# The first scores and the product with w_in of two row halves, issued head by head in turn, in a fused attention, SoLU and expert kernel

## The chip, the cores and the metric

The kernel runs on one core of one Trainium2 chip. The metric is the device time of one execution in microseconds (us). The core has TensorE (PE, with its weight loads as PEld), VectorE (DVE), ScalarE (ACT), GpSimd (POOL) and SyncE (SP, which issues the transfers).

## The reference

Eight batches of eight heads of attention, in which 32 packed queries per head first attend to 576 keys, and the 576 tokens then attend to the 32 packed values; a dense layer with a SoLU and a layer norm; and a layer of eight experts of which each token takes one.

```python
def sm_attn(qq, kk, vv):
    s = scale * np.matmul(qq, kk.transpose(0, 1, 3, 2))
    s = s - np.max(s, axis=-1, keepdims=True)
    a = np.exp(s)
    a = a / (np.sum(a, axis=-1, keepdims=True) + 1e-09)
    return np.matmul(a, vv)
p_packed = sm_attn(p, k, v)           # [8, 8, 32, 64]
out = sm_attn(q, p_packed, p_packed)  # [8, 8, 576, 64]
...
h = x @ w_in                          # [4608, 512] @ [512, 1024]
...
return (ln @ w_out).astype(np.float32)
...
xe = x[mask]
h = np.maximum(xe @ w1[e], 0.0)
ye = h @ w2[e]
out[mask] = gate_w[mask, None] * ye
```

## The kernel before

The program has two parts. The first does attention, the dense layer and the gate, batch by batch; the second does the experts. The change touches the first part alone.

Each batch is a row of steps, and every step is a function with a letter: `P` (`packed`) computes the first scores, their softmax and the packed values; `S` (`scores2`) the second scores; `W` (`w_keys`) multiplies the packed values by w_in, so that the hidden units follow from the second softmax directly; `A` (`attnT`) transposes that softmax; `H` (`hidden`) makes the hidden units of a tile of 128 tokens and their norm; `T` (`lnT`) transposes them; `X` (`second`) multiplies by w_out; `G` (`gate`) picks the expert. A string of letters sets the order in which the steps are written, with P, S, W and A one batch ahead. In the first batch the steps `F`, `I` and `D` are mixed in: they fetch w_in and w_out as float64 words and decode them to float32 on ScalarE, VectorE and GpSimd (lines 105 to 123 and 154 to 156).

The written order is not the order on the engines: the program is built with a scheduler (`schedule_with_timeline_sim=True`, at the end) that moves instructions within each engine's stream when the program is built. On the chip each engine takes its stream in that order.

The eight heads of a batch are split in two halves: heads 0 to 3 lie on the lower 64 partitions and heads 4 to 7 on the upper 64 (`g` is the half, `c` the head in it). In the first scores a matmul takes 64 rows and 32 columns (the 32 packed queries of one head), and writes 32 partitions of the accumulator: the four heads of a half fill its 128 partitions. So one group is four matmuls, each with 288 of the 576 keys; `hf` is the half of the keys. The product with w_in is built alike, with 512 of 1024 columns in a group. A float32 matmul appears in the trace as two matmuls and two weight loads, so a group is 8 rows of each.

The accumulator (PSUM) is shared out in pools. `psa` has two tiles of one bank and serves the first scores, their transposes, the packed values, the second scores, the product with w_in and the gate. `psh` has two tiles of two banks (tag `h`) and serves the hidden units alone. A new tile of a pool waits until the last reader of the tile that it replaces is done.

In `packed` a half g takes two tiles of psa for its scores (one for each half of the keys). Each has a maximum of its own (line 172), the two are merged (line 174), and two exponentials with a sum each follow (line 178); then the transposes (line 184) and their copies to SBUF (lines 185 and 188). The second half begins when the first is through. In `w_keys` each group has a tile of psa, and is copied twice (lines 219 and 220) into a rounded and a remainder part.

Of the kernel before, what the change touches and what calls it, by code (L numbers as in the profile page):

```python
# [12 lines left out]
F32 = mybir.dt.float32  # L13
# [5 lines left out]
# The upper word of 2^-127, the float64 whose exponent is 0 in float32, as float32 bits.  # L19
F64_LEAST = float(np.array(0x38000000, np.uint32).view(np.float32))  # L20
AF = mybir.ActivationFunctionType
ALU = mybir.AluOpType
AX = mybir.AxisListType
# [3 lines left out]
B, H, S, D, NP = 8, 8, 576, 64, 32  # L27
DM, FF, E, FF2 = 512, 1024, 8, 1024
P = 128
NC = 4          # heads of one half of the partitions; also chunks of 128 in DM  # L30
NF = FF // P    # chunks of 128 in FF (and in FF2)
# [6 lines left out]
def f32(ap):  # L38
    return ap.bitcast(F32)
# [3 lines left out]
def fused_kernel(ctx: ExitStack, tc, qT, kT, pT, vm, vt, w_in, w_out, g_ln, w_gate, w1, w2, out):  # L43
# [21 lines left out]
    # ------------------------------------------------------------ attention and the first layer  # L65
    with ExitStack() as ph:
# [23 lines left out]
        # Buffers of later steps in which the 16 blocks of the two float64 arrays are decoded,  # L90
        # and whether GpSimd multiplies their lower words.
# [3 lines left out]
        def fetch(src, i):  # L95
            """Words of float64 values, with room to decode them: [P, pairs | pairs, 512]."""
            tag = room[i]
            if tag == "e":
                raw = p4.tile([P, 2, 512], I32, name=f"raw{i}", tag="e")
                t = p4.tile([P, 2, 512], I32, name=f"bits{i}", tag="e")  # L100
            else:
                both = p1.tile([P, 2, 2, 512], I32, name=f"raw{i}", tag=tag)
                raw, t = both[:, 0], both[:, 1]
            raw = raw.rearrange("p t n -> p (t n)")
            SY.dma_start(raw.bitcast(I64), src)
            return raw.rearrange("p (n w) -> p n w", w=2), t

        def decode(dst, words, through_pool):
            """dst = the float64 values as float32."""
            w, t = words  # L110
            lo, hi = w[:, :, 0], w[:, :, 1]
            a, b2 = t[:, 0], t[:, 1]
            A.activation(f32(a), f32(hi), AF.Abs)
            V.tensor_scalar(f32(a), f32(a), F64_LEAST, None, op0=ALU.max)
            V.tensor_scalar(b2, a, 3, 0x3FFFFFFF, op0=ALU.logical_shift_left, op1=ALU.bitwise_and)
            V.scalar_tensor_tensor(a, hi, -0x40000000, b2, op0=ALU.bitwise_and, op1=ALU.bitwise_or)  # L116
            V.tensor_scalar(b2, a, -0x800000, None, op0=ALU.bitwise_and)
            if through_pool:
                A.activation(f32(lo), lo.bitcast(U32), AF.Copy, scale=2.0**-52)
                G.tensor_tensor(f32(b2), f32(lo), f32(b2), op=ALU.mult)  # L120
            else:
                V.scalar_tensor_tensor(f32(b2), lo.bitcast(U32), 2.0**-52, f32(b2), op0=ALU.mult, op1=ALU.mult)
            G.tensor_tensor(dst, f32(a), f32(b2), op=ALU.add)
# [34 lines left out]
        def packed(b):  # L158
            """The packed values of every head, [k, d], by 4 heads on the partitions."""
            s = st[b]  # L160
            rz = sm.tile([P, 2], F32, name=f"rz_{b}", tag="rz")
            a1T = pa.tile([P, NT, 2, P], F32, name=f"a1T_{b}", tag="a1T")
            for g in range(2):
                r = slice(g * 64, g * 64 + 64)
                nm = sm.tile([P, 2], F32, name=f"nm_{b}_{g}", tag="nm")
                pss = []
                for hf in range(2):
                    ps = psa.tile([P, 512], F32, name=f"s1_{b}_{g}_{hf}", tag="a")
                    for c in range(NC):
                        T.matmul(ps[c * NP : (c + 1) * NP, :HALF], s["p"][r, c, :],  # L170
                                 s["k"][r, c, hf * HALF : (hf + 1) * HALF], start=True, stop=True)
                    V.tensor_reduce(nm[:, hf : hf + 1], ps[:, :HALF], axis=AX.X, op=ALU.max, negate=True)
                    pss.append(ps)
                V.tensor_tensor(nm[:, 0:1], nm[:, 0:1], nm[:, 1:2], op=ALU.min)
                a = p2.tile([P, S], F32, name=f"a1_{b}_{g}", tag="a1")
                z = sm.tile([P, 2], F32, name=f"z_{b}_{g}", tag="z")
                for hf in range(2):
                    A.activation(a[:, hf * HALF : (hf + 1) * HALF], pss[hf][:, :HALF], AF.Exp, bias=nm[:, 0:1],
                                 accum_out=z[:, hf : hf + 1])
                V.scalar_tensor_tensor(z[:, 0:1], z[:, 0:1], 1e-9, z[:, 1:2], op0=ALU.add, op1=ALU.add)  # L180
                V.reciprocal(rz[:, g : g + 1], z[:, 0:1])
# [25 lines left out]
        def w_keys(b):  # L207
            """The packed values times w_in."""
            s = st[b]
            s["wb_hi"] = pa.tile([P, 2, FF], F32R, name=f"wbh_{b}", tag="wbh")  # L210
            s["wb_lo"] = pa.tile([P, 2, FF], F32R, name=f"wbl_{b}", tag="wbl")
            for hf in range(2):
                for g in range(2):
                    r = slice(g * 64, g * 64 + 64)
                    cols = slice(hf * 512, hf * 512 + 512)
                    ps = psa.tile([P, 512], F32, name=f"wb_{b}_{g}_{hf}", tag="a")
                    for c in range(NC):
                        T.matmul(ps[c * NP : (c + 1) * NP, :], s["pp"][r, c, :], w_in_sb[r, c, cols], start=True, stop=True)  # L218
                    A.copy(s["wb_hi"][:, g, cols], ps)
                    V.tensor_sub(s["wb_lo"][:, g, cols], ps, f32(s["wb_hi"][:, g, cols]))  # L220
# [44 lines left out]
        def hidden(b, t):  # L265
            """Hidden units of a tile of tokens, their SoLU and its layer norm (w_out carries the gain).

            With u = exp(h - max) h / FF and Z the softmax's denominator, SoLU is u FF / Z:
            its norm is (u - mean u) (var u + 1e-6 (Z / FF)^2) ^ -0.5.
            """  # L270
# [30 lines left out]
        def lnT(b, t):  # L301
# [8 lines left out]
            for f0 in (0, 4):  # L310
                # No other step of the first batch needs psx so early.
# [79 lines left out]
        # A step of the orders below is its letter, its part and, in the first one, a + for batch 1.  # L391
# [10 lines left out]
        # Every batch overlaps the first steps of the next one and the last steps of the one before.  # L402
# [7 lines left out]
    # ------------------------------------------------------------ the experts  # L410
    with ExitStack() as ph:
# [31 lines left out]
        def expert(xh, xl, b, e, emit, nm, split=()):  # L443
            """The terms of expert e for the tokens of batch b; emit(dc, halves, sums, weights) takes them.

            In the chunks of split one half of the tokens is done before the other.
            """
# [35 lines left out]
        # Each batch with the expert of its first token.  # L483
# [12 lines left out]
        # Where a token of any batch goes to another expert, its weight there is zero:  # L496
        # then all batches are computed again with all experts.
# [57 lines left out]
```

## Time and profile before

| | |
|---|---|
| time, median of 3 runs | 968.62 us (967.9 to 969.72) |
| profiled execution, span from first to last instruction | 967.9 us |
| TensorE busy | 915.5 us, 95% |
| VectorE, ScalarE, GpSimd busy | 56%, 42%, 13% |
| first part ends, second part begins | about 570 us |

The span of the profiled execution and the lowest of the three runs are the same to 0.1 us. A busy TensorE is not TensorE at its peak: matmuls overlap, so the time of a piece of work is read from its first start to the start of what comes next. The names of tiles in the trace are cut: `s` stands for first and second scores (lines 170 and 231), `wb` for the product with w_in, `a` for a softmax, `nm` for the maxima of the first scores, `lt` for the transposes of the hidden units, `x` for the product with w_out.

### The profile page before, as it was taken

Reading aid. Unit: us, or ns where it says so; the run is one execution under the profiler, and the core shown is the slowest. Engines: PE = TensorE matmul, PEld = TensorE weight load, DVE = VectorE, ACT = ScalarE, POOL = GpSimd, SP = SyncE. Lnnn points to the kernel's source line nnn. Section 1 sums busy time; section 2 is a strip of 40 time slices with the busy share of each in tenths; the row PEclk is TensorE's granted clock in tenths of the full one; section 3 lists DMA queues with packets and bytes.
Section 4 is the critical chain, followed back from the end, with each engine's and each line's share of the span. In section 5 each row is a group of like instructions: output and inputs, shape, how many; then the busy total and the mean of one; then the engine's idle time right before and its main releaser. Section 6 shows DMA issues by size and latency. Waiting matters only on the chain.

```text
span 967.9 us, 18591 instructions
## 1 busy us (share of the span) xinstructions
PE 915.5 (95%) x7480; PEld 807.3 (83%) x7480; DVE 539.3 (56%) x1090; ACT 402.2 (42%) x800; POOL 124.2 (13%) x228
## 2 busy tenths in 40 slices
PE   4466999999999999999999999999999999999997
PEld 1234777887878878788788999999999999999997
DVE  5999758575575756757456243353434353535331
ACT  4447555444554446444345241333323232324230
POOL 2776312011120101101010000000000000000000
PEclk9988999999999999999999999999999999999999
DMA  9613113022221222200106235353535353433411
GB/s 341 244 45 123 50 56 145 14 90 100 102 98 40 82 82 98 99 2 2 50 1 225 78 116 166 99 175 90 182 99 174 102 173 103 149 127 100 132 46 52
DMA packets 42506, 102.89 MB, mean 106 GB/s; under 512 B 4592, under 2 KB 14384, under 8 KB 38320
## 3 DMA queue, kind: packets, MB, share of 16 engines
q1 hardware_dynamic: 42416, 101.65, 31.1%
q8 instruction: 61, 1.00, 0.4%
q14 instruction: 29, 0.24, 0.1%
HBM read 82.60 MB, written 19.04 MB: 105 GB/s over the span
## 4 chain that ended last, share of the span: by engine, by line
PE 87%; DVE 6%; DMA 2%; ACT 1%; issue 1%; SPq 1%; POOL 0%; DVEq 0%; ACTq 0%
PE y L476 21%; PE x L331 21%; PE h L458 21%; PE h L279 11%; PE lt L315 3%; PE wb L218 2%; PE s L170 2%; PE s L231 2%; PE lg L342 1%; PE pp L193 1%; PE at L260 1%; DMA raw_0a<-w 1%; DVE raw L116 1%; PE a1t L184 1%; DVE e L298 1%
## 5 line engine op out<-in xcount | busy, mean ns | idle before, releaser
L331 PE MATMUL x<-lh,wo_hi 128*128 128x320 f32 (+1 forms) x512 | 155.8, 304 | 0.2 <-ACT x L333 0.2
L331 PE MATMUL x<-lh,wo_lo 128*128 128x320 f32 (+1 forms) x512 | 152.5, 298 | 0.0
L331 PE MATMUL x<-ll,wo_hi 128*128 128x320 f32 (+1 forms) x512 | 152.4, 298 | 0.0
L331 PEld LDWEIGHTS x<-lh,wo_hi 128*128 128x128 f32 x512 | 96.7, 189 | 18.6 <-issue 7.4
L331 PEld LDWEIGHTS x<-ll,wo_hi 128*128 128x128 f32 x512 | 96.9, 189 | 3.9 <-issue 2.5
L331 PEld LDWEIGHTS x<-lh,wo_lo 128*128 128x128 f32 x512 | 96.8, 189 | 2.2 <-issue 0.8
L318 DVE TENSOR_TENSOR ll<-lt,lh 128x512 fp32r<-128x512 f32 (+1 forms) x80 | 50.5, 632 | 47.7 <-ACT lh L317 47.6
L279 PE MATMUL h<-wbh,ath 128*128 128x512 f32 (+1 forms) x160 | 68.3, 429 | 6.6 <-DVE e L289 5.9
L281 DVE TENSOR_REDUCE hm<-h 128x1 f32<-128x512 f32 (+1 forms) x80 | 54.3, 685 | 26.2 <-PE h L279 25.7
L279 PE MATMUL h<-wbh,atl 128*128 128x512 f32 (+1 forms) x160 | 65.2, 408 | 0.0
L279 PE MATMUL h<-wbl,ath 128*128 128x512 f32 (+1 forms) x160 | 64.6, 404 | 0.0
L317 ACT CAST lh<-lt 128x512 fp32r<-128x512 f32 (+1 forms) x80 | 43.1, 540 | 46.4 <-PE lt L315 45.8
L489 DVE TENSOR_TENSOR o<-y,gb 128x576 f32<-128x576 f32 (+1 forms) x33 | 24.4, 739 | 67.7 <-PE y L476 65.6
L289 DVE SCALAR_TENSOR_TENSOR e<-e,h 128x1024 f32<-128x1024 f32 (+1 forms) x40 | 48.6, 1215 | 19.9 <-ACT e L287 19.9
L292 ACT ACTIVATE sq<-e,mu 128x1024 bf16<-128x1024 f32 (+1 forms) x40 | 46.0, 1150 | 22.1 <-DVE e L289 17.0
L287 ACT ACTIVATE e<-h,hm 128x1024 f32<-128x1024 f32 (+1 forms) x40 | 44.6, 1115 | 24.8 <-DVE hm L282 24.5
L333 ACT COPY x<-x 128x256 f32<-128x256 f32 (+1 forms) x64 | 25.4, 397 | 62.4 <-PE x L331 62.2
L315 PE MATMUL lt<-ident,e 128*128 128x128 f32 (+1 forms) x320 | 48.5, 271 | 0.9 <-DVE ll L318 0.9
L464 DVE SCALAR_TENSOR_TENSOR hl<-h,hh 128x576 fp32r<-128x576 f32 x64 | 47.8, 749 | 0.3 <-ACT hh L463 0.2
L315 PEld LDWEIGHTS lt<-ident,e 128*128 128x128 f32 (+1 forms) x320 | 35.9, 142 | 9.1 <-issue 4.4
L279 PEld LDWEIGHTS h<-wbh,ath 128*128 128x128 f32 (+1 forms) x160 | 29.8, 186 | 15.5 <-DVE e L289 7.1
L298 DVE TENSOR_SCALAR e<-e,mu,va 128x1024 f32<-128x1024 f32 (+1 forms) x40 | 35.3, 882 | 11.3 <-POOL va L297 10.5
(239 smaller groups left out, 2172.5 us busy)
## 6 DMA issues: line engine op xcount, KB each, us to landing
k<-kT SPq DMA_DIRECT2D x16, 576.0 KB
q<-qT SPq DMA_DIRECT2D x8, 1152.0 KB
x2s<-x SPq DMA_DIRECT2D x8, 1152.0 KB
x<-x2s SPq DMA_DIRECT2D x8, 1152.0 KB
yT<-o SPq DMA_DIRECT2D x31, 288.0 KB
v<-vm SPq DMA_DIRECT2D x8, 1024.0 KB
raw<-w_in SPq DMA_DIRECT2D x8, 512.0 KB
raw<-w_out SPq DMA_DIRECT2D x8, 512.0 KB
```

Source lines behind the costliest of these rows:

```text
L279: T.matmul(ps[:rows, cols], s[x][:, t, g, :rows], s[y][:, g, cols], start=(n == 0), stop=(n == len(passes) - 1))
L281: V.tensor_reduce(nm[:rows, hf : hf + 1], ps[:rows, cols], axis=AX.X, op=ALU.max, negate=True)
L287: A.activation(er, psr, AF.Exp, bias=nm[:rows, 0:1], accum_out=z[:rows])
L289: V.scalar_tensor_tensor(er, er, 1.0 / FF, psr, op0=ALU.mult, op1=ALU.mult, accum_out=mu[:rows])
L292: A.activation(sq[:rows], er, AF.Square, bias=mu[:rows], scale=-float(FF), accum_out=va[:rows])
L298: V.tensor_scalar(er, er, mu[:rows], va[:rows], op0=ALU.add, op1=ALU.mult)
L315: T.transpose(ps[:, fc, :rows], e[:rows, (f0 + fc) * P : (f0 + fc + 1) * P], ident[:rows, :rows])
L318: V.tensor_sub(s["ll", part][:, f0 : f0 + 4, t0 - p0 : t0 - p0 + rows], ps[:, :, :rows], f32(hi))
L331: T.matmul(ps[:, :pn], w[:, fc, cols], s[x, part][:, fc, :], start=(n == 0), stop=(n == 3 * NF - 1))
L458: T.matmul(ps[:, hf, :HALF], w[:, dc, :], x[:, dc, hf * HALF : (hf + 1) * HALF], start=(n == 0), stop=(n == 3 * NC - 1))
L464: V.scalar_tensor_tensor(lo, ps[:, :, :HALF], 0.0, f32(hi), op0=ALU.max, op1=ALU.subtract)
L476: T.matmul(ps[:, hf, :HALF], w[:, fc % 4, :], x[fc][:, hf, :], start=(n == 0), stop=(n == 3 * NF - 1))
```

## The change

In `packed` the scores of both halves are made first, head by head with the halves in turn, into two tiles of `psh`; a half's 576 columns then lie in the two banks of one tile, so one maximum, one exponential and one sum serve them all. In `w_keys` the groups of both halves are made together, head by head in turn, into the two tiles of `psa`. The comments and docstrings that the new file also drops stand for nothing in the program.

```diff
         def packed(b):
...
+            pss = [psh.tile([P, 2, 512], F32, name=f"s1_{b}_{g}", tag="h") for g in range(2)]
+            for hf in range(2):
+                for c in range(NC):
+                    for g in range(2):
+                        r = slice(g * 64, g * 64 + 64)
+                        T.matmul(pss[g][c * NP : (c + 1) * NP, hf, :HALF], s["p"][r, c, :],
+                                 s["k"][r, c, hf * HALF : (hf + 1) * HALF], start=True, stop=True)
             for g in range(2):
-                r = slice(g * 64, g * 64 + 64)
-                nm = sm.tile([P, 2], F32, name=f"nm_{b}_{g}", tag="nm")
-                pss = []
-                for hf in range(2):
-                    ps = psa.tile([P, 512], F32, name=f"s1_{b}_{g}_{hf}", tag="a")
-                    for c in range(NC):
-                        T.matmul(ps[c * NP : (c + 1) * NP, :HALF], s["p"][r, c, :],
-                                 s["k"][r, c, hf * HALF : (hf + 1) * HALF], start=True, stop=True)
-                    V.tensor_reduce(nm[:, hf : hf + 1], ps[:, :HALF], axis=AX.X, op=ALU.max, negate=True)
-                    pss.append(ps)
-                V.tensor_tensor(nm[:, 0:1], nm[:, 0:1], nm[:, 1:2], op=ALU.min)
+                nm = sm.tile([P, 1], F32, name=f"nm_{b}_{g}", tag="nm")
+                V.tensor_reduce(nm, pss[g][:, :, :HALF], axis=AX.XY, op=ALU.max, negate=True)
                 a = p2.tile([P, S], F32, name=f"a1_{b}_{g}", tag="a1")
-                z = sm.tile([P, 2], F32, name=f"z_{b}_{g}", tag="z")
-                for hf in range(2):
-                    A.activation(a[:, hf * HALF : (hf + 1) * HALF], pss[hf][:, :HALF], AF.Exp, bias=nm[:, 0:1],
-                                 accum_out=z[:, hf : hf + 1])
-                V.scalar_tensor_tensor(z[:, 0:1], z[:, 0:1], 1e-9, z[:, 1:2], op0=ALU.add, op1=ALU.add)
-                V.reciprocal(rz[:, g : g + 1], z[:, 0:1])
+                z = sm.tile([P, 1], F32, name=f"z_{b}_{g}", tag="z")
+                A.activation(a.rearrange("p (h n) -> p h n", h=2), pss[g][:, :, :HALF], AF.Exp, bias=nm, accum_out=z)
+                V.tensor_scalar_add(z, z, 1e-9)
+                V.reciprocal(rz[:, g : g + 1], z)
...
         def w_keys(b):
...
             for hf in range(2):
+                cols = slice(hf * 512, hf * 512 + 512)
+                ps = [psa.tile([P, 512], F32, name=f"wb_{b}_{g}_{hf}", tag="a") for g in range(2)]
+                for c in range(NC):
+                    for g in range(2):
+                        r = slice(g * 64, g * 64 + 64)
+                        T.matmul(ps[g][c * NP : (c + 1) * NP, :], s["pp"][r, c, :], w_in_sb[r, c, cols], start=True, stop=True)
                 for g in range(2):
-                    r = slice(g * 64, g * 64 + 64)
-                    cols = slice(hf * 512, hf * 512 + 512)
-                    ps = psa.tile([P, 512], F32, name=f"wb_{b}_{g}_{hf}", tag="a")
-                    for c in range(NC):
-                        T.matmul(ps[c * NP : (c + 1) * NP, :], s["pp"][r, c, :], w_in_sb[r, c, cols], start=True, stop=True)
-                    A.copy(s["wb_hi"][:, g, cols], ps)
-                    V.tensor_sub(s["wb_lo"][:, g, cols], ps, f32(s["wb_hi"][:, g, cols]))
+                    A.copy(s["wb_hi"][:, g, cols], ps[g])
+                    V.tensor_sub(s["wb_lo"][:, g, cols], ps[g], f32(s["wb_hi"][:, g, cols]))
```

What the scheduler makes of it is seen at three places. The first is TensorE in the middle of the first part, where the product with w_in of one batch meets the first scores of batch 6; `wb_1_0` is the upper half's group with the first 512 columns. Before, the order there is:

```order
L315 MATMUL lt_2_0_3775<-ident,e_2_3610 128x128 x4
L218 MATMUL wb_1_0_3829<-w_in_sb,ppc_3326 32x512 x4
L218 MATMUL wb_0_1_3836<-w_in_sb,ppc_3326 32x512 x4
L331 MATMUL x_4_0_0_4157<-lh_0_3577,wo_hi 128x256
L331 MATMUL x_4_0_0_4157<-ll_0_3578,wo_hi 128x256
```

After the change the groups of the second columns stand head by head in turn, and scores of batch 6 right behind them (three more pairs like the first two rows stand ahead of these):

```order
L215 MATMUL wb_0_1_3788<-w_in_sb,ppc_3278 32x512
L215 MATMUL wb_1_1_3789<-w_in_sb,ppc_3278 32x512
L169 MATMUL s_6_1_3902<-k_3490,p_3487 32x288 x6
L169 MATMUL s_6_0_3901<-k_3490,p_3487 32x288
L169 MATMUL s_6_1_3902<-k_3490,p_3487 32x288
```

The scores of the two halves, `s_6_0` and `s_6_1`, are in turn in their last matmuls only. Six of the lower half's eight stand earlier in the stream, behind `wb_1_0`:

```order
L277 MATMUL h_4_3741<-wbh_3054,atl_3133 64x512
L215 MATMUL wb_1_0_3775<-w_in_sb,ppc_3278 32x512 x4
L169 MATMUL s_6_0_3901<-k_3490,p_3487 32x288 x6
L329 MATMUL x_3_1_3_3685<-lh_1_3007,wo_hi 128x320
L329 MATMUL x_3_1_3_3685<-ll_1_3008,wo_hi 128x320
```

So of a batch's four groups of wb one has stayed alone (`wb_0_0`, earlier in the stream), one has moved ahead of six matmuls of the scores, and two stand in turn with the rest of the scores behind them; before, the scores stood apart, four and four matmuls of one half in a row.

The second place is TensorE in the start, behind the packed values of batch 0 (`ppT` is their transpose). Before, the second scores of batch 0 and then the product with w_in follow:

```order
L198 MATMUL ppT_255<-ident,pn_253 128x128
L231 MATMUL s_0_1_261<-bd_121,q_136 64x2x32 x16
L231 MATMUL s_0_0_288<-bd_121,q_136 64x2x32 x16
L231 MATMUL s_0_2_325<-bd_121,q_136 64x2x32 x4
L218 MATMUL wb_0_0_424<-w_in_sb,ppc_257 32x512 x4
L218 MATMUL wb_1_0_431<-w_in_sb,ppc_257 32x512 x4
```

After, the first scores of batch 1, whose halves do stand in turn, come between them:

```order
L195 MATMUL ppT_247<-ident,pn_245 128x128
L229 MATMUL s_0_1_253<-bd_121,q_136 64x2x32 x16
L229 MATMUL s_0_0_280<-bd_121,q_136 64x2x32 x16
L169 MATMUL s_1_0_568<-k_390,p_387 32x288
L169 MATMUL s_1_1_569<-k_390,p_387 32x288
```

These scores have moved ahead of the product with w_in of batch 0; before the change they stand behind the first hidden units.

The third place is VectorE in the start. Before, the maxima of batch 1's first scores come behind those of the hidden units (line 281):

```order
L281 TENSOR_REDUCE hm_0_711<-h_0_710 128x1
L281 TENSOR_REDUCE hm_1_795<-h_1_794 128x1
L172 TENSOR_REDUCE nm_0_576<-s_1_0_0_577 128x1
L172 TENSOR_REDUCE nm_0_576<-s_1_0_1_583 128x1
L174 TENSOR_TENSOR nm_0_576<-nm_0_576 128x1
L114 TENSOR_SCALAR raw_452<-raw_452 128x512
L281 TENSOR_REDUCE hm_0_711<-h_0_710 128x1
```

After, they stand among the decode of the weights (`raw`, `bits`):

```order
L173 TENSOR_REDUCE nm_0_586<-s_1_0_568 128x1
L116 SCALAR_TENSOR_TENSOR raw_346<-raw_346 128x512
L173 TENSOR_REDUCE nm_1_602<-s_1_1_569 128x1
L240 TENSOR_REDUCE z_0_2_327<-a_0_2_324 64x8
L241 TENSOR_SCALAR z_0_0_302<-z_0_0_302 128x16
L116 SCALAR_TENSOR_TENSOR bits_383<-raw_382,bits_383 128x512
L218 TENSOR_TENSOR wbl_415<-wb_0_0_416,wbh_414 128x512
L117 TENSOR_SCALAR raw_346<-raw_346 128x512
```

They have moved ahead of the first remainder of the product with w_in (line 218 of the new file), and there is one maximum for a half in place of two and a merge.

## Rows read from the trace of the kernel before

**Rows 1.** The profile's page: busy us of the engines, share of the span.
```profile
PE 915.5 (95%) x7480; PEld 807.3 (83%) x7480; DVE 539.3 (56%) x1090; ACT 402.2 (42%) x800; POOL 124.2 (13%) x228
```

**Rows 2.** Three stretches: length, busy us of PE, PEld, DVE, ACT, POOL; granted clock.
```profile
20.00:62.00 42.00, 19.88 (x151) 10.18 (x140) 41.92 (x63) 18.67 (x36) 33.06 (x23) 1.00 0.52 180
62.00:100.00 38.00, 27.67 (x261) 19.72 (x262) 34.54 (x69) 26.62 (x53) 25.98 (x32) 0.82 0.31 104
100.00:570.00 470.00, 467.73 (x4039) 382.57 (x4038) 287.35 (x668) 226.25 (x487) 61.47 (x166) 1.00 0.22 76
```

**Rows 3.** TensorE's waits: total us, number of times, the longest.
```profile
PE s L231 <- DVE a L239: 6.8, 1, 6.8
PE ppT L198 <- DVE pn L196: 6.1, 1, 6.1
PE h L279 <- DVE e L289: 5.9, 3, 2.8
PE s L170 <- DVE atl L263: 4.4, 1, 4.4
```

**Rows 4.** All waits of VectorE from 18.6 to 62 us.
```profile
DVE bits L114 <- ACT bits L113: 0.2, 1, 0.2
```

**Rows 5.** TensorE in order of time, one group of the product with w_in.
```profile
276.44 1.06 PE L218 MATMUL wb<-w_in_sb,ppc 64*32 64x512 f32 x8
277.43 0.41 PE L331 MATMUL x<-lh,wo_hi 128*128 128x320 f32 x1
```

**Rows 6.** TensorE in order of time, two such groups in a row.
```profile
281.58 1.09 PE L218 MATMUL wb<-w_in_sb,ppc 64*32 64x512 f32 x16
282.60 0.39 PE L331 MATMUL x<-lh,wo_hi 128*128 128x256 f32 x1
282.82 0.28 PE L331 MATMUL x<-ll,wo_hi 128*128 128x256 f32 x1
282.94 0.28 PE L331 MATMUL x<-lh,wo_lo 128*128 128x256 f32 x1
```

**Rows 7.** First 0.12 us of both, instructions of line 218 alone.
```profile
276.44:276.56 0.12, 0.12 (x4) 0.12 (x8) 1.00 0.00 0
...
281.58:281.70 0.12, 0.12 (x8) 0.12 (x16) 1.00 0.00 0
```

**Rows 8.** TensorE, the first scores of one half's four heads, all columns.
```profile
241.76 1.18 PE L170 MATMUL s<-k,p 64*32 64x288 f32 x16
242.87 0.38 PE L331 MATMUL x<-lh,wo_hi 128*128 128x256 f32 x1
```

**Rows 9.** Groups of instructions by line: busy us, mean ns, idle before.
```profile
L172 DVE TENSOR_REDUCE nm<-s 128x1 f32<-128x288 f32 x32 | 14.5, 454 | 10.9 <-PE s L170 10.7
L281 DVE TENSOR_REDUCE hm<-h 128x1 f32<-128x512 f32 (+1 forms) x80 | 54.3, 685 | 26.2 <-PE h L279 25.7
L287 ACT ACTIVATE e<-h,hm 128x1024 f32<-128x1024 f32 (+1 forms) x40 | 44.6, 1115 | 24.8 <-DVE hm L282 24.5
L289 DVE SCALAR_TENSOR_TENSOR e<-e,h 128x1024 f32<-128x1024 f32 (+1 forms) x40 | 48.6, 1215 | 19.9 <-ACT e L287 19.9
```

**Rows 10.** ScalarE in order of time, the start; idle before in brackets.
```profile
15.18 0.50 ACT L178 ACTIVATE a<-s,nm 128x288 f32<-128x288 f32 x1 [2.86 <-DVE nm L174]
17.89 0.69 ACT L113 ACTIVATE bits<-raw 128x512 f32<-128x512 f32 x1
```

**Rows 11.** VectorE in order of time, the start.
```profile
8.48 0.46 DVE L172 TENSOR_REDUCE nm<-s 128x1 f32<-128x288 f32 x1 [1.24 <-PE s L170]
8.97 0.16 DVE L174 TENSOR_TENSOR nm<-nm 128x1 f32<-128x1 f32 x1
9.77 0.43 DVE L115 TENSOR_SCALAR raw<-raw 128x512 int32<-128x512 int32 x1
18.62 0.43 DVE L114 TENSOR_SCALAR bits<-bits 128x512 f32<-128x512 f32 x1 [0.16 <-ACT bits L113]
```

**Rows 12.** A stretch of the start with its granted clock.
```profile
65.00:70.00 5.00, 4.96 (x23) 2.90 (x24) 3.26 (x8) 2.86 (x8) 4.41 (x4) 0.50 0.28 99
```

## The prediction

> **What bounds the kernel now.** The page comes first: TensorE is busy for 95% of the span [rows 1]. The three stretches then show where it is not [rows 2]: from 100 to 570 us it is busy for 467.7 of 470 us, from 20 to 62 for 19.9 of 42, and from 62 to 100 for 27.7 of 38. In the first of these early stretches VectorE is busy for 41.9 of 42 us, and its list of waits there has one entry of 0.2 us [rows 4]. TensorE's longest waits are all for VectorE [rows 3]. So there are two regimes. In the **start**, up to about 96 us, VectorE's queue (the decode of the weights, mixed with batch 0) sets the pace, and faster matmuls are worth nothing. In the **steady stretch** after it TensorE never waits, and each microsecond of TensorE's stream that goes is a microsecond of the kernel. The experts' part is not touched.
>
> **What two halves cost side by side.** The trace of before already holds both cases. One group of wb alone takes from 276.44 to 277.43: 0.99 us [rows 5]. At 281.58 the scheduler happened to set `wb_1_0` and `wb_0_1` next to each other, one of the upper and one of the lower rows: both are through at 282.60, in 1.02 us [rows 6]. In the first 0.12 us eight of their matmuls have started, against four of the single group [rows 7]. So groups of different row halves run side by side for 0.03 us, and they need not be written in turn: standing next to each other is enough. Two groups of one half do not: the scores of one half, two groups on the same rows, take 241.76 to 242.87, 1.10 us [rows 8], which is four passes. With some 0.135 us around a burst, a pass of the scores is (1.10 - 0.135) / 4 = 0.24 us, and one of wb (0.99 - 0.135) / 2 = 0.43 us. A burst of such groups then lasts as long as its longest chain of passes on one place (one row half, one head), plus 0.135, plus 0.03 if both halves are in it.
>
> The Trainium skill has a rule here (TensorE: Matmul & The Clock Gate, Part 3, What overlaps and what doesn't): a weight load overlaps running matmuls only where its row group differs. By it the order in turn would matter by itself, since only a matmul of the other half could cover a load, and a lone group would expose its loads. The single group's row shows all eight loads of one row half begun within 0.12 us, while its first four matmuls run [rows 7], so here the rule doesn't hold and adjacency alone counts. By the rule each burst in turn would gain some 0.1 to 0.2 us more, 1 us in all; the sum below goes by the row.
>
> **Steady stretch, burst by burst.** The order shows that the scheduler undoes much of the written order. For a regular batch (the product of one, the scores of the next):
> - before: `wb_0_0` alone 0.99, `wb_1_0` with `wb_0_1` 1.02, `wb_1_1` alone 0.99, the scores twice 1.10: 5.20 us.
> - after: `wb_0_0` alone 0.99; `wb_1_0` with six matmuls of `s_0` (four passes of scores on the lower rows, two of wb on the upper) 4 x 0.24 + 0.165 = 1.13; the last two groups of wb in turn with the ten other matmuls of the scores behind them (two passes of wb, then four of scores on the upper rows) 2 x 0.43 + 4 x 0.24 + 0.165 = 1.99: 4.11 us.
>
> That is 1.1 us a batch and not the 2 us that the diff suggests. Counted like this over all bursts from the product of batch 1 on, 36 bursts before make 36.3 us and 25 after make 32.4: **-3.8 us**. The irregular batches gain least: in batch 3, `s_3_0` is torn into pieces of 6, 1 and 1.
>
> A change between shapes costs too: the second x comes 0.22 us after the first behind a burst, the third 0.12 [rows 6], so about 0.09 a change. In the whole order changes between shapes fall from 320 to 310 (26 fewer around bursts, 16 more among transposes, hidden units and x): **-0.9 us**.
>
> **Start.** Three terms.
> - VectorE loses work. Per half the two maxima of 0.46 and the merge of 0.16 [rows 9, 11] become one maximum over 576 columns. No row has that; from 288 columns at 454 ns and 512 at 685 ns [rows 9] it is 1.03 ns a column, so 0.75 us. The sum of the exponential keeps one small instruction. That is 0.32 us a half, four halves in the start: -1.3 us.
> - The second half no longer waits for the first. ScalarE idles 2.86 us for the second half's maximum [rows 10], and the first block's decode on VectorE that counts, at 18.62, waits for ScalarE's step at 17.89 [rows 10, 11]. But in the new order both maxima stand behind line 115 of the first block, which ends at 10.20, where the first half's second maximum began at 8.48 [rows 11]: 1.7 us of the 2.9 are given back. -1.1 us.
> - Batch 1's first scores move ahead of batch 0's product with w_in, and with them two maxima and four small instructions on VectorE, 2 x 0.75 + 4 x 0.15 = 2.1 us, queued ahead of the remainders of wb for which the second softmax and the hidden units wait. They are taken out of the stretch from 62 to 100, where VectorE is busy for 34.5 of 38 us [rows 2]: at nine tenths busy most of it comes back. I take +0.4.
>
> Together **-2.0 us**. The bounds: behind its 4.4 us wait [rows 3] TensorE takes batch 1's scores at the lower clock, twice 1.10, and the other half's 1.10 later [rows 8]; if nothing takes their place there, these go as well, and the start gains 5.5. If the 2.1 us don't come back and TensorE loses 2.5 us more to the clock, it loses 4: from 65 to 70 us it is busy for 4.96 of 5 us at a granted 0.50, 1.2 in place of 2.4 GHz [rows 12], and a longer wait may bring one more such stretch.
>
> Costed at nothing: the exponentials and sums on ScalarE (226 of 470 us busy [rows 2]), VectorE's lighter load in the steady stretch, and the wait for both tiles of psa in `w_keys` (the last group before a pair stands 24 x and a burst earlier).
>
> **Sum.** 967.9 - 3.8 - 0.9 - 2.0 = 961.2 us against the profiled execution. The median stands 0.7 us above that: **962 us**.
>
> **Rivals.**
> - *The halves share the hidden units' banks (slower).* The scores now take both tiles of `psh`, so the upper half's scores wait for the last hidden tile `h_4` of the batch before. The Trainium skill warns of it (TensorEngine Tiling (Array Packing), Restrictions and Gotchas, PSUM Pressure): row tiles need banks of their own. The price: the tile is free after the maximum 0.69, a small merge, the exponential 1.12 and the product 1.22 [rows 9], some 3.3 us. The cover in the new order: the burst of 1.13, 24 x of 320 columns (0.12 for 256 [rows 6], so 0.15), and the two passes of wb ahead of the scores, some 5.6 us. So it begins once VectorE comes 2.3 us late to `h_4`; it is busy for 61% [rows 2]. From there each microsecond costs six; at 1.6 us more it takes back the whole gain and 3 us besides, 971 us.
> - *The start gives it back (no change).* The VectorE queue ahead of wb is longer by 2.1 us and batch 0's hidden units come later; with the lower clock this costs up to 4 us, and the sum is 967 to 970. For it: the start is a chain of a scheduler's choices. Against: VectorE has less to do in all.
> - *All halves side by side (faster still).* The Trainium skill promises this (the same page, Theoretical Speedup): with 64 rows and 32 columns eight tiles work at once. By these rows a batch would take 1.13 + 2 x 1.02 = 3.17 us, 2.0 less than before, some 14 in all: 951 us. The order speaks against it.
> - *Alternation breaks the overlap.* If each change of row half drained the array, the 16 passes of a pair of wb would follow one another, 6.9 us in place of 1.0, in five bursts some 29 us: 990 us. Against it: sixteen matmuls of two halves in 1.02 us [rows 6].
>
> **How the numbers follow.** Forecast (957 to 966.7) 0.74, all side by side 0.03, start gives back 0.13, shared banks 0.08, alternation 0.02. Within 0.2% (966.7 to 970.6) is no change, about what a measurement here can tell: faster 0.77, same 0.13, slower 0.10. The range holds eight in ten: the start's gain bound with the rest gives 957.7, its loss bound 968.
>
> **What would show it.** Right: bursts of `wb` and `s` of 0.99, 1.13 and 1.99 us in the steady batches, TensorE still without waits there, VectorE's first busy stretch from about 17.5 us. Wrong: waits of `s` for the product of line 289 (shared banks), or x of batch 0 starting later than 99 us (start).

## The result and the profile after

The changed kernel takes 977.27 us (median of 5 runs, 973.3 to 979.44) against 968.62 us: a ratio of 1.008 (95% interval 1.0057 to 1.0103). It is slower by 0.8%, where 962 us was forecast and 968 was the range's upper end. The profiled execution has a span of 976.8 us against 967.9.

The page of the changed kernel, busy time of the engines [rows 1], and the third of the stretches of [rows 2]:

```profile
PE 918.3 (94%) x7480; PEld 813.9 (83%) x7480; DVE 540.0 (55%) x1058; ACT 396.0 (41%) x768; POOL 122.8 (13%) x228
```

```profile
100.00:570.00 470.00, 463.23 (x3979) 383.78 (x3972) 288.47 (x646) 221.53 (x459) 69.15 (x172) 0.98 0.21 73
```

TensorE is busy for 2.8 us more in all, although its stream was to become shorter. From 100 to 570 us it is busy 4.5 us less than before, at a clock of 0.98 and not 1.00. So there is a loss in a stretch that the prediction held to be full.

**The steady batches did what was forecast.** TensorE in order of time, one regular batch of the changed kernel, and the first burst of the next batch:

```profile
342.81 1.06 PE L215 MATMUL wb<-w_in_sb,ppc 64*32 64x512 f32 x8
343.80 0.41 PE L329 MATMUL x<-lh,wo_hi 128*128 128x320 f32 x1
...
349.34 0.63 PE L215 MATMUL wb<-w_in_sb,ppc 64*32 64x512 f32 x4
...
350.46 0.42 PE L329 MATMUL x<-lh,wo_hi 128*128 128x320 f32 x1
...
354.60 1.09 PE L215 MATMUL wb<-w_in_sb,ppc 64*32 64x512 f32 x16
355.49 1.17 PE L169 MATMUL s<-k,p 64*32 64x288 f32 x20
356.59 0.38 PE L329 MATMUL x<-lh,wo_hi 128*128 128x256 f32 x1
...
400.89 1.06 PE L215 MATMUL wb<-w_in_sb,ppc 64*32 64x512 f32 x8
```

The bursts, each read from its first row to the next x, take 0.99, 1.12 and 1.99 us; 0.99, 1.13 and 1.99 were forecast. A batch takes 400.89 - 342.81 = 58.08 us. In the kernel before, the group at 276.44 [rows 5] returns at 336.10, 59.66 us later. So a batch is 1.58 us shorter. TensorE in the kernel before, the first hidden unit of batch 3 and that group, and then the first hidden unit of batch 3 after the change:

```profile
237.99 0.48 PE L279 MATMUL h<-wbh,ath 128*128 128x512 f32 x1
...
336.10 1.06 PE L218 MATMUL wb<-w_in_sb,ppc 64*32 64x512 f32 x8
```

```profile
253.00 0.48 PE L277 MATMUL h<-wbh,ath 128*128 128x512 f32 x1
```

The hidden units of batch 3 begin 15.0 us later than before, the experts' part only 8.9 us later (533.1 against 524.2): all that is lost is lost ahead of batch 3, and the steady batches then give 6 us of it back.

**The loss lies between 93 and 185 us.** The products with w_out (x) need all eight blocks of w_out, whose last step on GpSimd is line 156. That line in the kernel before, then in the changed one (count, duration, first and last start):

```profile
L156 POOL TENSOR_TENSOR wo_lo<-wor,wo_hi x8: 1266/1290/1537, 60.4 to 99.4; 128x512 fp32r<-128x512 f32 x8
```

```profile
L156 POOL TENSOR_TENSOR wo_lo<-wor,wo_hi x8: 1271/1284/1529, 66.4 to 116.4; 128x512 fp32r<-128x512 f32 x8
```

The last block is 17 us late. The first x starts only 2.8 us later (102.0 against 99.2 us), but it stops after 18 of its 24 matmuls, with six of eight blocks. TensorE hardly waits for the two others (0.6 us, in the list below): in its order other work follows the 18th matmul, and the next x stands behind that, at 116.4 us. Three stretches of 8 us, x matmuls alone (line 331; busy us of PE and PEld), before:

```profile
100.00:108.00 8.00, 5.41 (x43) 5.00 (x42) 1.00 0.39 147
108.00:116.00 8.00, 4.20 (x27) 3.24 (x25) 1.00 0.01 2
116.00:124.00 8.00, 3.43 (x24) 3.21 (x24) 1.00 0.00 0
```

and after (line 329):

```profile
100.00:108.00 8.00, 4.21 (x18) 3.91 (x18) 0.57 0.30 128
108.00:116.00 8.00, 0.00 (x0) 0.00 (x0) 0.85 0.50 156
116.00:124.00 8.00, 2.02 (x6) 1.43 (x6) 0.51 0.01 2
```

96 of these matmuls have begun by 124 us before (a row also counts those that run on from the row above), 24 after. Batch 1's first hidden unit still comes at the same time as before (119.4 against 119.2 us), but the x left undone have to run behind it, and batch 2's begins at 195.0 against 178.3. With few x, TensorE has mainly the next batch's chain of steps, and waits for it. Its waits from 92 to 190 us after the change (7.8 us in all with one of 0.2; before, two of 0.5 and 0.2 us):

```profile
PE lg L340 <- ACT x L331: 2.0, 1, 2.0
PE at L258 <- DVE wbl L218: 1.7, 1, 1.7
PE wb L215 <- DVE wbl L218: 1.4, 1, 1.4
PE lt L313 <- DVE ll L316: 1.0, 1, 1.0
PE h L277 <- DVE e L287: 0.9, 1, 0.9
PE x L329 <- POOL wo_lo L156: 0.6, 1, 0.6
```

By an estimate the larger part goes to the clock. Three stretches of the changed kernel, all engines:

```profile
93.20:106.80 13.60, 12.71 (x61) 7.54 (x59) 13.35 (x24) 5.45 (x10) 6.64 (x9) 0.50 0.24 87
113.65:123.90 10.25, 7.95 (x29) 6.26 (x28) 7.26 (x15) 7.04 (x16) 3.57 (x7) 0.50 0.10 30
181.90:185.30 3.40, 3.40 (x18) 3.40 (x17) 0.14 (x1) 0.00 (x0) 0.00 (x0) 0.50 0.55 228
```

TensorE is busy there for 24.1 us at a granted 0.50, 1.2 GHz. Its x follow one another 0.21 us apart then (102.40, 102.62, 102.83 us) and 0.12 us apart at 1.00 [rows 6]. If all of the 24.1 us slowed like x, 44% of it, 10.5 us, is the price, an estimate. The fair comparison is run 5 below, which has all of the change and w_out in time. From 92 to 190 us, all engines, the changed kernel and then run 5:

```profile
92.00:190.00 98.00, 90.38 (x692) 66.48 (x693) 62.66 (x137) 45.04 (x94) 22.95 (x42) 0.86 0.21 75
```

```profile
92.00:190.00 98.00, 96.02 (x902) 76.39 (x901) 69.80 (x154) 56.92 (x118) 23.79 (x48) 1.00 0.22 75
```

TensorE is without work for 7.6 us here and for 2.0 in run 5, where the clock is full throughout. In run 5 the hidden units of batch 3 begin at 234.8 us, 18.2 us earlier than here. The 10.5 us of the clock and the 5.6 us of further waits make 16 of these 18.2; the rest is open.

**Why the last block is late.** VectorE's first and last of the four steps of the last block, in the kernel before and then in the changed one:

```profile
87.26 0.41 DVE L114 TENSOR_SCALAR raw<-raw 128x512 f32<-128x512 f32 x1
...
88.89 0.43 DVE L117 TENSOR_SCALAR raw<-raw 128x512 int32<-128x512 int32 x1
```

```profile
90.98 0.41 DVE L114 TENSOR_SCALAR raw<-raw 128x512 f32<-128x512 f32 x1
...
102.41 0.41 DVE L117 TENSOR_SCALAR raw<-raw 128x512 int32<-128x512 int32 x1
```

The block is 3.7 us late at the first step and 13.5 us at the end of the last (102.82 against 89.32), since steps of batches 0, 1 and 2 now stand between the four. That is most of the 17 us. The rest is added behind it, on ScalarE above all. ScalarE in order of time in the changed kernel (L154 and L155 are the two steps of w_out's last two blocks, L217 copies batch 1's product with w_in), and GpSimd's step ahead of L154:

```profile
107.98 0.58 ACT L217 CAST wbh<-wb 128x512 fp32r<-128x512 f32 x1 [5.24 <-PE h L277]
...
110.70 0.58 ACT L217 CAST wbh<-wb 128x512 fp32r<-128x512 f32 x1 [1.82 <-PE wb L215]
111.18 0.72 ACT L154 ACTIVATE wor<-wor,g_sb 128x512 f32<-128x512 f32 x1
...
112.79 0.73 ACT L154 ACTIVATE wor<-wor,g_sb 128x512 f32<-128x512 f32 x1
...
115.70 0.62 ACT L155 CAST wo_hi<-wor 128x512 fp32r<-128x512 f32 x1
```

```profile
104.92 2.85 POOL L123 TENSOR_TENSOR wor<-raw 128x512 f32<-128x512 f32 x2
```

The first of the two blocks is ready for ScalarE at about 106.4 us (half of GpSimd's row). ScalarE does nothing then: it idles 5.24 us up to 107.98 and 1.82 us up to 110.70 for TensorE's steps, whose evictions stand ahead of L154 in its queue. The Trainium skill (Perfetto Trace Analysis, Tensor Engine Instruction) says that ScalarE, VectorE and GpSimd take their queues strictly in order; the rows agree. In the kernel before, ScalarE did the two blocks' four steps from 92.12 to 98.80 us, ahead of all of batch 1's product. On both engines the order of steps was chosen by the scheduler.

### The profile page after: what moved, and what is told of

The parts are those of the page before. It is cut to its first block, busy times and chain, and to the rows that moved or that the text cites. A ratio compares the mean times of both kernels' runs of the same rounds, so it can differ in the third digit from the quotient of the medians.

```text
span 976.8 us, 18501 instructions
## 1 busy us (share of the span) xinstructions
PE 918.3 (94%) x7480; PEld 813.9 (83%) x7480; DVE 540.0 (55%) x1058; ACT 396.0 (41%) x768; POOL 122.8 (13%) x228
## 4 chain that ended last, share of the span: by engine, by line
PE 87%; DVE 5%; DMA 4%; ACT 1%; SPq 1%; issue 1%; POOL 0%
PE x L329 21%; PE y L474 21%; PE h L456 20%; PE h L277 11%; PE lt L313 3%; PE wb L215 2%; PE s L229 2%; PE s L169 1%; PE lg L340 1%; PE pp L190 1%; DMA raw<-w_in 1%; DMA p<-pT 1%; PE at L258 1%; DVE raw L116 1%; DMA raw_0a<-w 1%; DVE raw L114 1%
## 5 line engine op out<-in xcount | busy, mean ns | idle before, releaser
L329 PE MATMUL x<-lh,wo_lo 128*128 128x320 f32 (+1 forms) x512 | 154.8, 302 | 0.6 <-POOL wo_lo L156 0.6
L215 PE MATMUL wb<-w_in_sb,ppc 64*32 64x512 f32 x256 | 36.0, 672 | 11.9 <-DVE wbl L218 5.7
L313 PEld LDWEIGHTS lt<-ident,e 128*128 128x128 f32 (+1 forms) x320 | 35.6, 141 | 10.2 <-issue 5.0
```

Source lines behind the costliest of these rows:

```text
L215: T.matmul(ps[g][c * NP : (c + 1) * NP, :], s["pp"][r, c, :], w_in_sb[r, c, cols], start=True, stop=True)
L313: T.transpose(ps[:, fc, :rows], e[:rows, (f0 + fc) * P : (f0 + fc + 1) * P], ident[:rows, :rows])
L329: T.matmul(ps[:, :pn], w[:, fc, cols], s[x, part][:, fc, :], start=(n == 0), stop=(n == 3 * NF - 1))
```

## The experiments

**1. The scores alone.** The product with w_in is written as before, one tile at a time.

```diff
-                ps = [psa.tile([P, 512], F32, name=f"wb_{b}_{g}_{hf}", tag="a") for g in range(2)]
...
+                for g in range(2):
...
+                    ps = psa.tile([P, 512], F32, name=f"wb_{b}_{g}_{hf}", tag="a")
```

> The changed kernel with the product with w_in written as before (one group after another, one tile at a time); only the first scores are changed. Theory A (batch 1's first scores now run ahead of batch 0's product with w_in, and their two maxima and small steps stand ahead of its remainders on VectorE; the late hidden units bring TensorE gaps and the lower clock up to 190 us): the scores still move ahead, so the loss stays: 973 to 981 us. Theory B (the product in turn wants both tiles of psa at once, so its second pair waits for two evictions in VectorE's full queue): the loss in the start goes, the steady gain stays: 958 to 966 us. Theory C (the upper half's scores wait for the hidden units' banks): as the changed kernel, 973 to 981 us.

Measured: 977.77 us, 1.0085 [1.0068, 1.0101], the last L156 at 116.5 us. The pair of tiles (B) is not the cause, and the product's edit doesn't show in the time (a batch, from the first hidden unit of batch 3 to that of batch 7 and divided by four, takes 58.48 us against 58.09 in the changed kernel). Applied alone to the kernel before, it leaves the compiled order of all five engines row for row as it was: the scheduler un-does the turns.

**2. Batch 0 in the old form.**

```diff
+        def packed(b):
+            (packed_old if b < 1 else packed_new)(b)
...
+        def w_keys(b):
+            (w_keys_old if b < 1 else w_keys_new)(b)
```

> The changed kernel, but batch 0 takes both steps in the form of before. In the order batch 1's first scores still stand ahead of batch 0's product with w_in. Theory A: the loss stays, 972 to 980 us. Theory B: batch 0's product is in the old form and batch 1's is not, so at most half of the loss stays, 962 to 969 us. A fourth theory D (batch 0's own softmax of the packed keys is what comes late in VectorE's queue): it is back in the old form, so the loss goes, 958 to 964 us.

Measured: 960.58 us, 0.9916 [0.9899, 0.9932], although batch 1's scores still run ahead of batch 0's product. Theory A falls. Theory D had the number right, but D alone doesn't say why; the last L156 starts at 99.5 us here.

**3. Batch 1's scores in the old form**, the rest as changed.

```diff
+            (packed_old if b == 1 else packed_new)(b)
```

> The changed kernel, but batch 1 alone takes its first scores in the form of before, in psa; the product with w_in stays in turn in every batch. In the order batch 1's first scores are back behind batch 0's first hidden units, and batch 0's product stands ahead of them. Theory A: the loss in the start goes and the steady gain of 1.57 us a batch stays: 957 to 965 us. Theory B: nothing about the pair of tiles has changed, 973 to 981 us. Theory C: batches 2 to 7 still use the hidden units' banks, and what was lost behind batch 1 stays lost: 970 to 978 us.

Measured: 966.0 us, 0.9969 [0.9958, 0.9981], between what A and C gave. Batch 0 is in the new form, so D isn't the cause either: two different edits cure most of the loss. C falls with this run and the next, in which the shared banks stay. Why this run takes some 4 us more than runs 2 and 4 is open; the difference is there when batch 3 begins (238.98 us, against 234.12 and 236.06).

**4. Batches 0 and 1 in the old form**, in both steps.

```diff
+            (packed_old if b < 2 else packed_new)(b)
...
+            (w_keys_old if b < 2 else w_keys_new)(b)
```

> The changed kernel, but batches 0 and 1 take both steps in the form of before. The order is that of the kernel before up to batch 0's second tile of transposed hidden units (about 95 us). Theories A, B and D alike put the loss into the first two batches: the first x of batch 2 some 1 to 2 us earlier than in the kernel before, and six steady batches at 1.57 us less each, 957 to 963 us. Theory C: the six batches that share the banks keep their waits, 968 us or more.

Measured: 962.42 us, 0.9928 [0.9911, 0.9944]. The gain of the later batches is real and C is refuted.

What runs 2 to 4 share is the last L156, at 99.5, 98.0 and 98.2 us; in the changed kernel and in run 1 it is at 116.4 and 116.5. From this comes theory E, the next expectation.

**5. The last block of w_out early.** One word; all of the change stays.

```diff
-        room = "lh0 ll0 lh1 ll1 e e x2 lh0 ll0 lh1 ll1 e lh1 ll1 x2 lh1".split()
+        room = "lh0 ll0 lh1 ll1 e e x2 lh0 ll0 lh1 ll1 e lh1 ll1 x2 e".split()
```

> The changed kernel with one word of the table of decode buffers changed: the sixteenth block of weights (the last of w_out) is decoded in two buffers of the hidden units and need not wait for the thirteenth. Everything of the change stays (scores in the banks of the hidden units, both halves in turn, batch 1's scores ahead of batch 0's product with w_in). In the order both last blocks of w_out now stand ahead of batch 1's product on ScalarE, as in the kernel before. Theory E (what was lost is that the last two blocks of w_out come 15 to 17 us later, behind batch 1's product with w_in and batch 2's first scores in VectorE's and ScalarE's queues, so that TensorE has no products with w_out to fill its waits between 93 and 124 us): w_out whole by about 100 us and 957 to 964 us. Theory A (batch 1's scores ahead) or C (shared banks): 972 us or more.

Measured: 961.83 us, 0.9925 [0.9908, 0.9942]: 15.4 us less than the changed kernel (the kernel before, run beside it, took 969.40). Line 156 and the x matmuls in this run, to be held against the rows above:

```profile
L156 POOL TENSOR_TENSOR wo_lo<-wor,wo_hi x8: 1275/1280/1464, 66.8 to 100.9; 128x512 fp32r<-128x512 f32 x8
```

```profile
100.00:108.00 8.00, 3.14 (x24) 2.93 (x24) 1.00 0.02 7
108.00:116.00 8.00, 3.88 (x24) 3.28 (x25) 1.00 0.07 9
116.00:124.00 8.00, 3.19 (x24) 3.12 (x25) 1.00 0.43 149
```

x begins at 103.4 us, later than in the changed kernel, but then goes on: 72 of them have begun by 124 us, and the clock stays at 1.00. The word moves more than the blocks: some 6% of TensorE's instructions stand elsewhere in its order than in the changed kernel (3% in run 9). So this run is to be read with the others that bring w_out in time by other edits.

**6. The same word in the kernel before.**

> The kernel before with the same one word of the table changed, as a control: w_out was whole at about 100 us there already. Theory E: little to gain, 964 to 970 us, so that the difference to the run above is the steady gain of 7 to 9 us. If the word alone is worth 8 us or more here too (961 us or less), the run above says nothing on theory E.

Measured: 970.69 us, 1.0014 [1.0005, 1.0024]. The word is worth nothing by itself. Against this control the change, with w_out in time, gains 970.69 - 961.83 = 8.9 us.

**7. The last two blocks late in the kernel before.**

```diff
+            if fc >= 6:
+                late = sm.tile([P, 1], F32, name=f"late{fc}", tag="late")
+                G.tensor_scalar(late, f32(st[1]["wb_hi"][:, 0, fc : fc + 1]), 0.0, 0.0, op0=ALU.mult, op1=ALU.add)
+                G.tensor_tensor(late, late, gc, op=ALU.add)
+                gc = late
...
+                if i == 0 and step == "W":
+                    decode_w_out(7, words[15])
+                    decode_w_out(6, words[14])
```

> The kernel before, with the gain of the last two blocks of w_out made to wait for batch 1's product with w_in (two small instructions on GpSimd make the factor from one column of that product, times zero), so that both are whole some 12 us later; first scores and product are in the old form. Theory E: the loss of the changed kernel shows without any of its edits: 974 to 982 us. Theory A or C, or a loss through the lower clock that the waits for VectorE bring by themselves: within 968 to 972 us.

Measured: 972.61 us, 1.0035 [1.002, 1.0049], the last L156 (line 161 here) at 110.2 us. The sign is E's and the size is not: 3.2 us, where at least 5 were expected. The delay is 10.8 us and not 17, and behind 95 us TensorE spends 3.4 us at the lower clock (105.0 to 108.5), where the changed kernel spends 25. Nor does this delay take away as many x: 61 have begun by 124 us, where the changed kernel has 24.

**8. Not in turn**: four heads of the lower rows, then four of the upper.

```diff
-                for c in range(NC):
-                    for g in range(2):
+                for g in range(2):
+                    for c in range(NC):
```

> The changed kernel, but in both steps the four heads of the lower rows are written first and then the four of the upper, in the same banks and with the same one maximum. In the order the last two blocks of w_out stand behind batch 1's product here too. Theory E and the burst model (neighbours overlap whether in turn or not): 973 to 981 us, and bursts of the same length in the steady batches (a pair of wb 1.0 to 1.1 us). If turns matter by themselves, pairs of wb take 1.8 us or more and the time is 5 us or more above the changed kernel, 982 us or more.

Measured: 973.84 us, 1.0049 [1.0033, 1.0066], the last L156 at 114.9 us. A pair of groups of the product, written one after the other (TensorE in order of time):

```profile
347.66 1.09 PE L215 MATMUL wb<-w_in_sb,ppc 64*32 64x512 f32 x16
348.56 0.64 PE L169 MATMUL s<-k,p 64*32 64x288 f32 x7
```

The next instruction starts 0.90 us later, 0.89 in the changed kernel (354.60 and 355.49). Adjacency is enough, as [rows 6] said. By the Trainium skill's rule (TensorE: Matmul & The Clock Gate, Part 3, What overlaps and what doesn't) the loads of four heads on one row half could not overlap; a pair out of turn would then be longer, and it isn't.

**9. The last block in another buffer.**

```diff
-        room = "lh0 ll0 lh1 ll1 e e x2 lh0 ll0 lh1 ll1 e lh1 ll1 x2 lh1".split()
+        room = "lh0 ll0 lh1 ll1 e e x2 lh0 ll0 lh1 ll1 e lh1 ll1 x2 ll0".split()
```

> As run 5, but the sixteenth block is decoded in another buffer that comes free between the two (that of the second and ninth block): in the order the last block but one of w_out stands behind the first evicted half of batch 1's product, the rest ahead of it, so that w_out should be whole between run 5 (102.2 us) and the changed kernel (117.7 us). Theory E: the time lies between these two too and goes with the moment at which w_out is whole: 961 to 969 us. If only run 5's particular order was lucky: 972 us or more.

Measured: 961.82 us, 0.9925 [0.9908, 0.9941], the last L156 at 104.8 us. 4 us of delay against run 5 cost nothing; the first x starts at 103.5 us here, and 65 have begun by 124.

**10. Early and not in turn**: the edits of runs 5 and 8 together.

> Run 8's kernel (lower rows' heads first, then the upper rows') with run 5's word of the table: w_out whole by about 100 us. Theory E: 959 to 966 us, that is 8 to 14 us below run 8, and within 3 us of run 5, since neighbours overlap in either order. If turns matter by themselves in the steady stretch, 5 us or more above run 5.

Measured: 964.8 us, 0.9959 [0.9944, 0.9973], 9.0 us below run 8, the last L156 at 97.4 us. The time is at the edge of the 3 us from run 5. Its batches (from the first hidden unit of batch 3 to that of batch 7, divided by four) take 58.88 us against 58.31 in run 5. The bursts of a regular batch are as long as in run 5; in one batch of the four the product is torn into 4 and 12 instructions.

**11. Both cures**: the edits of runs 2 and 5 together.

> Run 2 (batch 0 in the form of before) with run 5's word of the table, as a version that may beat all: both cures of the start at once. Theory E says that they are the same cure (w_out whole by about 100 us), so they don't add up: 957 to 963 us. If each had removed a loss of its own, they would add: 950 us or less.

Measured: 959.84 us, 0.9919 [0.9887, 0.9951]. They don't add up. This is the lowest median of all, but not told apart from runs 2, 5 and 9.

## Why the prediction was wrong, step by step

- *The bursts*: right, in kind and length. That turns by themselves count for nothing was right too: a pair takes 0.90 us out of turn and 0.89 in turn (run 8), and the 0.1 to 0.2 us a burst that the rule would have given does not show.
- *The steady gain*: the mechanism was right, the term too small. Of the 1.58 us a batch, 1.10 are the bursts, as worked out. The 0.9 us for changes between shapes were to give 0.1 us a batch; the rest is 0.48. The router's logits (lg) and their transposes (lgt) have more than that: in the new order the two groups of lg stand together and lgt comes later, with no wait. Before, lg takes 0.63 us twice and lgt, with a wait of 0.15 us, 0.97 us up to the next row, 2.23 us in all:

```profile
346.74 0.69 PE L342 MATMUL lg<-x,wg 128*32 128x288 f32 x8
347.37 0.66 PE L315 MATMUL lt<-ident,e 128*128 128x128 f32 x4
347.95 0.69 PE L342 MATMUL lg<-x,wg 128*32 128x288 f32 x8
348.58 0.44 PE L348 MATMUL lgt<-ident,lg 128*128 128x128 f32 x2
349.17 0.55 PE L348 MATMUL lgt<-ident,lg 128*128 128x128 f32 x3 [0.15 <-ACT lg L343]
349.55 0.38 PE L315 MATMUL lt<-ident,e 128*128 128x128 f32 x2
```

  and after the change 1.11 and 0.47 us, 1.58 us in all:

```profile
359.31 1.18 PE L340 MATMUL lg<-x,wg 128*32 128x288 f32 x16
360.42 0.39 PE L329 MATMUL x<-lh,wo_lo 128*128 128x256 f32 x1
...
361.78 0.71 PE L346 MATMUL lgt<-ident,lg 128*128 128x128 f32 x5
362.25 0.37 PE L329 MATMUL x<-lh,wo_hi 128*128 128x256 f32 x1
```

  In all, 4.7 us were forecast for the two terms and 6.7 with the start; runs 5 and 6 show 8.9 us for the change where w_out is in time.
- *The start*: this is the step that failed. Its small pieces held: a maximum takes 0.74 us (0.75 worked out), and VectorE's first full stretch begins at 16.93 us, where 18.62 was before [rows 11] and 17.5 forecast. But the sum of -2.0 counted only what comes ahead of the first x. For batch 1's scores I asked what they are put in front of (the product with w_in, +0.4 us) and left out what falls behind: the decode of w_out, on which the x depend that fill TensorE's stream here. In place of +0.4 us, batch 0's hidden units begin 8.6 us later (63.64 against 55.06), w_out's last block comes 17 us later, and some 18 us are lost by batch 3. The 8.6 us are not the loss: in run 5, which gains, batch 0's hidden units begin at 63.84. The bound of +4 us allowed one more stretch at the lower clock; three came. Nor do the bounds follow from their terms: -1.3 - 1.1 + 2.1 + 2.5 makes a loss of 2.2 and not of 4, and 957.7 leaves out the 0.7 us that the other end, 968, has.
- *The rival "the start gives it back"* had the place and the sign, and the price wrong: 4 us at most, where some 18 us were lost. The sign set for it, x of batch 0 after 99 us, is true in this kernel (102.0), in run 5 (103.4), which gains, and even in the kernel before (99.23): the right sign was whether x, once begun, goes on.
- *Shared banks*: refuted by runs 4, 5 and 9; from 190 to 510 us run 4 has no wait of TensorE. *All halves side by side* didn't come about, as the order said (its eight tiles stand in the Trainium skill under TensorEngine Tiling (Array Packing), Available Configurations), and *alternation* breaks nothing (the pairs above).

**What is shown and what is open.** That the late blocks bring the loss is shown by where the times fall. The seven runs in the new form that have the last L156 by 104.8 us (2, 3, 4, 5, 9, 10 and 11), by different edits, take 959.8 to 966.0 us; the three that have it from 114.9 us on (the changed kernel, 1 and 8) take 973.8 to 977.8. Run 5 does it with all of the change in place, and run 6 excludes that its word does it by itself. Run 7 is the weak point: a delay of the blocks alone, forced on the kernel before, costs 3.2 us and not the 5 or more expected. The x that have begun by 124 us put it near the runs without the loss: 24 in the changed kernel and in run 1, 35 in run 8, 61 in run 7, and 65 to 96 in the seven. That fits the account, but was seen after the runs and not tested. The split into waits and clock is an estimate from one trace. Runs 7 and 8 have less of the lower clock too (3.4 and 10.2 us behind 95 us), so it may decide on the size, but no run kept the delay and changed the clock alone. The changed kernel's five executions spread from 973.3 to 979.4 us and don't follow their mean clock (0.971 and 0.983 at these two). Why the scheduler sets the last blocks so late in just these orders was not tried.

## What to carry to other kernels

Where a scheduler sets the order, a change at one step is priced by what falls behind it as well as by what it moves ahead of; look for the last input of the work that fills the bounding engine's waits. Ask not when such filler begins but when its last block is there. And when a change with a sound gain comes out slower, move the suspected late input alone: here one word of a buffer table made a loss of 8.7 us a gain of about 7.

## What was not expected of the hardware

- A long stretch at the lower clock can cost next to nothing. Run 5 has TensorE at a granted 0.50 from 31 to 72 us, busy for 19.1 of 41 us beside a full VectorE. Of its four executions the one with a mean clock of 0.997 took 961.06 us, the others, with 0.972 to 0.975, 961.29 to 963.04; in run 6 five executions with 0.973 to 0.978 took 970.20 to 971.16 us and five with 0.990 to 0.994 took 969.14 to 972.07. Where the clock was low in the executions without a trace is not known. The 27 us behind 93 us in the changed kernel, for 24.1 of which TensorE is busy, cost some 10 by the estimate above.
- TensorE was full and stayed at the lower clock: in the changed kernel it is busy for 8.00 of 8 us from 100 to 108, at a granted 0.57.
- The same VectorE step takes 0.41 or 1.5 us in the start. VectorE in order of time, kernel before:

```profile
31.24 1.50 DVE L115 TENSOR_SCALAR bits<-bits 128x512 int32<-128x512 int32 x1
...
35.94 0.41 DVE L115 TENSOR_SCALAR raw<-raw 128x512 int32<-128x512 int32 x1
```

  During the first, GpSimd is busy throughout (30.99 to 33.85 us), at the start of the second it is idle (33.85 to 36.15). The Trainium skill (SBUF — State Buffer, SBUF: two separate sides) says that the two engines share a pair of ports, which a GpSimd step or a VectorE step in its two-port mode holds for the whole instruction while the other waits; the rows agree with it, and no run tested it. If it is so, VectorE's load in the start depends on the order as well as on its work.
